# Two ScalarE steps of a weight chunk issued half a block later, and a 384-column copy given to GpSimd, in an attention and mixture-of-experts kernel

## Chip, cores and metric

The kernel runs on one core of one Trainium2 chip. The metric is the device time of one execution in microseconds (us); the figure given for a kernel is the median of its runs.

## What is computed

The reference is a strided attention followed by two dense stages. Cut to what matters:

```python
def reference(q, k, v, w1, w2, w3, w_out, probs, e_w1, e_w2):
    attn = masked_softmax(q @ k.T / 8) @ v       # 2 batches, 8 heads, 576 rows, 64 per head
    x = attn as a (1152, 512) matrix             # 1152 tokens
    h = ((x @ w1) * (x @ w2)) @ w3               # 512 -> 1024 -> 1024
    x3 = h @ w_out                               # 1024 -> 512
    p = probs / (probs.sum(-1) + 1e-9)
    return sum(p[:, e:e+1] * (relu(x3 @ e_w1[e]) @ e_w2[e]) for e in range(4))
```

## The kernel before

TensorE multiplies in a rounded 32-bit format, so every operand is split into a high part (the rounded value) and a low part (the rest), and each product is three matmuls (L305 high by high, L306 and L307 the two mixed terms). The weights w1, w2, w_out and w3 arrive as 64-bit numbers and are turned into 32-bit ones on the chip.

**Weight chunks.** There are 20 of them, in this order: eight of w1 and w2 together (c_w12), four of w_out, eight of w3. A chunk passes through these steps, each on 128 x 1024 elements:

- a DMA loads it (L140, SyncE's queue); it is issued by load_next, which add calls, so that the load of the chunk two places on is issued behind this chunk's add;
- ScalarE: round_up (L144, works on the low words), then magnitude (L149, writes the tile t). These are the "first two ScalarE steps" of the change, called the **words** below;
- VectorE: clamp (L185, reads and writes t), shift (L188), sign (L191), add (L195, needs the low words of L144);
- the split: split_hi (L203, ScalarE), then split_lo (L232, VectorE).

The generator work() (L260 to L291) issues these steps in a fixed order for one chunk after another. Each call of advance takes it one yield further. The four yields of a chunk c are: split_hi of the chunk before and clamp of c; split_lo of the chunk before and shift of c; sign of c; the words of the chunk after c, then add of c.

**Blocks.** The products a = x @ w1 and b = x @ w2 are made in 32 units (16 for each batch; a unit is one of eight column groups ft by one half, 288 tokens, of a batch). ab_block (L578) issues a unit in two halves. First half: 12 matmuls for a and a ScalarE copy out of PSUM to the tile ab (L601). Second half: 12 matmuls for b and the VectorE product of it with ab (L603). The rest of the unit is issued during the next unit: split_hi (L549, ScalarE, reads the product of L603) at the start of the next unit's first half, split_lo (L553, VectorE) at the start of its second half. Each half has one PSUM bank, taken in turn from five (pool ps). A bank is free again when L601 or L603 has read it.

run_unit (L881 to L898) sets the order, once per half:

```python
for _ in range(2):
    next(rest, None)      # L549 or L553 of the unit before
    next(block)           # matmuls, then L601 or L603
    if done >= 2:
        advance(1)        # one step of work()
```

Every engine's instructions run in the order in which the program issues them. In the second batch (units 16 to 31) steps of work() begin again with unit 18: the clamp of chunk w_out 1 stands in its first half. From there a chunk's four yields fill two units, clamp always in the first half of an even unit and add (with the next chunk's words) in the second half of an odd one. The chunks clamped in units 18, 20, 22, 24, 26, 28 and 30 are w_out 1, 2, 3 and w3 0, 1, 2, 3.

After units 17, 20 and 23 ab_split (L555) splits a pair of whole products of the first batch: ScalarE L562 and L563, VectorE L566 and L567. ab_place (L522) reserves a buffer for split products; for the last pair of the second batch, at the start of unit 28, it also copies 2 x 192 columns of the first batch's products from one buffer to another (L529, ScalarE). They are read in the third stage, by x3_block.

After unit 31 come eight products w3 by w_out (wc_tile, L618; accumulators from the same five banks; product number it needs chunk w3 it), then x3_block and the experts.

Of the kernel before, what the change touches and what calls it, by code (L numbers as in the profile page):

```python
# [8 lines left out]
F32 = mybir.dt.float32  # L9
# [18 lines left out]
MID = 384  # L28
# [16 lines left out]
def kernel(  # L45
# [13 lines left out]
    nc = tc.nc  # L59
# [192 lines left out]
    def load_next(held=False):  # L252
        nonlocal loaded
        if loaded < len(stream):
            stream[loaded].raw_load(held)
            loaded += 1
            for load in rest_loads.pop(loaded, ()):
                load()

    def work():  # L260


        wide = stream[2:20]
        before = None
        for c, after in zip(wide, wide[1:] + [None]):
            if before:
                while live > 14:
                    yield False
                before.split_hi()
            c.clamp()  # L270
            yield True
            if before:
                before.split_lo()
            c.shift()
            yield True
            c.sign()
            yield True
            if after:
                after.round_up()
                after.magnitude()  # L280
            c.add()
            yield True
            before = c
        while live > 14:
            yield False
        before.split_hi()
        yield True
        before.split_lo()
        yield True
        for w in c_e:  # L290
            yield from w.work()  # L291

    worker = work()

    def advance(n=1):

        return all([next(worker, False) for _ in range(n)])

    def need(c, part=0):
        while not (c.done if part == 0 else c.done1 if part == 1 else c.done2):  # L300
            assert advance()
# [218 lines left out]
    parts_of, middle, whole = {}, {}, {}  # L520

    def ab_place(b, pair):  # L522
        both = big[b].tile([P, 4 * S], F32R, tag="big", name="ab_parts")
        parts_of[b, pair] = both[:, :4 * MAIN].rearrange("p (x k n) -> p x k n", x=2, k=2)
        rest = both[:, 4 * MAIN:].rearrange("p (x n) -> p x n", x=2)
        if pair == 3 and b == 0:
            middle[pair, 0] = rest[:, :, MID // 2:]
        elif pair == 3:
            nc.scalar.copy(rest[:, :, :MID // 2], middle[pair, 0].bitcast(F32))  # L529
        middle[pair, 1 - b] = rest  # L530

    def ab_pieces(b, ft, t0, n):
# [22 lines left out]
    def ab_split(pair):  # L555

        ab_place(0, pair)
        if (1, pair) not in parts_of:
            ab_place(1, pair)
        ab, main = whole.pop(pair), parts_of[0, pair]  # L560
        for k in range(2):
            nc.scalar.copy(middle[pair, k][:, 0, :MID // 2], ab[:, k, MAIN:])  # L562
        nc.scalar.copy(main[:, 0], ab[:, :, :MAIN])  # L563
        for k in range(2):
            x = middle[pair, k][:, :, :MID // 2]
            nc.vector.tensor_tensor(out=x[:, 1], in0=ab[:, k, MAIN:], in1=x[:, 0].bitcast(F32), op=ALU.subtract)  # L566
        nc.vector.tensor_tensor(out=main[:, 1], in0=ab[:, :, :MAIN], in1=main[:, 0].bitcast(F32), op=ALU.subtract)  # L567
# [10 lines left out]
    def ab_block(b, ft, n):  # L578
        t = slice(b * S + n * HB, b * S + n * HB + HB)
        pair, late = ft // 2, b == 0 and ft < 6  # L580
        ab = tmp.tile([P, HB], F32, tag="pT", name="ab")
        if n == 0 and ft % 2 == 0:
            if late:
                if pair < 2:
                    parts = big[pair].tile([P, 2, 2, S], F32, tag="big", name="ab_f32")
                    whole[pair] = parts[:, 0]
                    if pair:
                        whole[2] = parts[:, 1]
            elif (b, pair) not in parts_of:
                ab_place(b, pair)  # L590
        if late:
            full = whole[pair][:, ft % 2, n * HB:n * HB + HB]
        else:
            full = ab
            pieces = ab_pieces(b, ft, n * HB, HB)
        for w in range(2):
            acc = bank("ab_acc")[:, :HB]
            for k in range(4):
                mm3(acc, c_w12[ft].parts((w * 4 + k) * P, P), (x_hi[:, k, t], x_lo[:, k, t]), k == 0, k == 3)
            if w == 0:  # L600
                nc.scalar.copy(ab, acc)  # L601
            else:
                nc.vector.tensor_tensor(out=full, in0=acc, in1=ab, op=ALU.mult)  # L603
            yield
        if late:
            return
        split_hi(pieces, ab)
        yield
        split_lo(pieces, ab)
        yield  # L610
# [132 lines left out]
    class Step:  # L743
# [22 lines left out]
        def add(self, out, acc, b):  # L766
            nc.vector.tensor_tensor(out=out, in0=acc, in1=b, op=ALU.add)  # L767

        def first(self, work):

            n = self.half.n
# [6 lines left out]
            self.product(b, "s2", "t2")  # L778
            self.add(u2, b, u1)
            work(1)  # L780
            self.product(c, "s3", "t3")
            self.add(u3, c, u2)
# [58 lines left out]
    def load_probs():  # L841
        den = const.tile([P, NTT], F32, name="den")
        nc.sync.dma_start(out=pn, in_=probs)
        nc.vector.tensor_reduce(out=den, in_=pn, axis=mybir.AxisListType.X, op=ALU.add)
        nc.vector.tensor_scalar_add(den, den, 1e-9)
        nc.vector.reciprocal(den, den)
        nc.vector.tensor_tensor(out=pn, in0=pn, in1=den.unsqueeze(2).to_broadcast([P, NTT, E]), op=ALU.mult)
# [4 lines left out]
    with tc.manual_schedule():  # L852
# [24 lines left out]
        rest = iter(())  # L877
# [3 lines left out]
        def run_unit():  # L881

            nonlocal done, rest
            b, ft, i = units[done]
            if done >= 2:
                need(c_w12[ft])
            block = ab_block(b, ft, i)
            for _ in range(2):
                next(rest, None)
                next(block)  # L890
                if done >= 2:
                    advance(1)
                if waiting:
                    waiting.pop().slots_exps()
            rest = block
            done += 1
            if b == i == 1:
                c_w12[ft].free()  # L898
# [139 lines left out]
        while done < 16:  # L1038
            if done == 3:
                need(c_w12[2])  # L1040
            run_unit()
            if done in (4, 5, 6, 7, 8, 10, 11, 13, 14):
                attend(1, next(steps))
            if done == 6:
                zero.whole_split()
        load_probs()
        while done < 32:
            run_unit()
            if done in (18, 21, 24):
                ab_split({18: 0, 21: 1, 24: 2}[done])  # L1050
        for _ in rest:
            pass
        for i in (loaded, loaded + 3):
            if i < 20:
                stream[i].spare = xp, "x_lo"
# [5 lines left out]
        for it in range(8):  # L1061
# [9 lines left out]
            if i is not None:  # L1071
                c = wc[i]
# [4 lines left out]
        c = None  # L1077
# [132 lines left out]
```

## Time and profile before

| what | us |
|---|---|
| median of 3 runs (lowest, highest) | 618.53 (618.53, 618.88) |
| the profiled execution | 618.26 |
| its span in the profile | 616.1 |
| TensorE busy in the span | 609.8 |
| VectorE busy | 443.1 |
| ScalarE busy | 280.6 |
| GpSimd busy | 9.9 |

The profiled execution lies 0.27 us below the median and 2.16 us above its own span. In the profile PE is TensorE's matmuls, PEld its weight loads, DVE VectorE, ACT ScalarE, POOL GpSimd, SP SyncE; L12 is line 12 of the kernel. A matmul's shown duration overlaps that of the next one, so its rate is read from start to start.

### The profile page before, as it was taken

The page shows a single profiled execution, that of the slowest core. Times are in us where ns is not written, and L with a number is a line of the kernel's source. Part 1 is how long each engine was busy: PE and PEld are TensorE (multiplying, and loading weights), DVE is VectorE, ACT ScalarE, POOL GpSimd, SP SyncE. Part 2 cuts the span into 40 slices and gives each one's busy share as a digit, 9 for nine tenths or more (in the row PEclk, how much of TensorE's full clock was granted, in tenths as well). Part 3 has the DMA queues.
Part 4 walks back from the last instruction along what each step waited for, and adds up shares of the span by engine and source line. Part 5 has one row for each costly group of instructions (what it writes and reads, how often), then busy time and mean ns, then how long its engine had stood idle before and what let it go on. Part 6 is the DMA issues. An engine that isn't in the chain of part 4 may idle for free.

```text
span 616.1 us, 11131 instructions
## 1 busy us (share of the span) xinstructions
PE 609.8 (99%) x4488; PEld 555.9 (90%) x4488; DVE 443.1 (72%) x811; ACT 280.6 (46%) x568; POOL 9.9 (2%) x33
## 2 busy tenths in 40 slices
PE   8999999999999999999999999999999999999997
PEld 5799999998889999998899988999889898989997
DVE  4899987998863237777877987887766665755843
ACT  3879966665733134333433333434343333333320
POOL 4100000000000000000000000000000000000000
PEclk9999999999999999999999999999999999999999
DMA  9896330334522202333545334435585557464411
GB/s 272 321 325 185 139 138 2 111 132 172 202 68 102 86 19 69 137 138 136 199 153 194 128 149 172 167 142 212 178 318 202 213 192 248 162 234 176 156 51 68
DMA packets 28510, 99.63 MB, mean 162 GB/s; under 512 B 2660, under 2 KB 6316, under 8 KB 26028
## 3 DMA queue, kind: packets, MB, share of 16 engines
q1 hardware_dynamic: 27916, 98.34, 44.5%
q8 instruction: 35, 0.57, 0.4%
q10 hardware_dynamic: 544, 0.59, 0.3%
q14 instruction: 15, 0.12, 0.1%
HBM read 79.78 MB, written 19.14 MB: 161 GB/s over the span
## 4 chain that ended last, share of the span: by engine, by line
PE 90%; DVE 4%; ACT 3%; DMA 2%; issue 1%; DVEq 0%; ACTq 0%; SPq 0%
PE g_acc L305 11%; PE g_acc L306 11%; PE g_acc L307 11%; PE m_a L307 4%; PE m_a L306 4%; PE m_a L305 4%; PE ab_acc L305 3%; PE ab_acc L307 3%; PE ab_acc L306 3%; PE m_b L306 3%; PE m_c L305 3%; PE m_c L306 3%; PE m_b L305 3%; PE x_acc L305 3%; PE m_c L307 3%; PE m_b L307 3%
## 5 line engine op out<-in xcount | busy, mean ns | idle before, releaser
L761 ACT ACTIVATE h_hi<-u 128x320 fp32r<-128x320 f32 (+1 forms) x128 | 56.9, 445 | 188.9 <-DVE u L767 188.9
L305 PE MATMUL g_acc<-w_hi,h_hi 128*128 128x512 f32 (+1 forms) x296 | 114.3, 386 | 0.0
L306 PE MATMUL g_acc<-w_lo,h_hi 128*128 128x512 f32 (+1 forms) x296 | 114.2, 386 | 0.0
L307 PE MATMUL g_acc<-w_hi,h_lo 128*128 128x512 f32 (+1 forms) x296 | 113.7, 384 | 0.0
L700 DVE TENSOR_TENSOR w_lo<-raw,w_hi 128x768 fp32r<-128x768 f32 x64 | 69.3, 1084 | 12.3 <-ACT w_hi L698 12.3
L767 DVE TENSOR_TENSOR u<-m_b,u 128x320 f32<-128x320 f32 (+1 forms) x96 | 40.7, 451 | 50.4 <-PE m_b L307 50.4
L305 PE MATMUL ab_acc<-x_hi,w_hi 128*128 128x288 f32 x240 | 71.6, 298 | 0.4 <-ACT ab L601 0.2
L307 PE MATMUL ab_acc<-x_hi,w_lo 128*128 128x288 f32 x240 | 70.7, 295 | 0.0
L306 PE MATMUL ab_acc<-x_lo,w_hi 128*128 128x288 f32 x240 | 70.7, 294 | 0.0
L307 PEld LDWEIGHTS g_acc<-w_hi,h_lo 128*128 128x128 f32 x296 | 55.6, 188 | 11.6
L305 PEld LDWEIGHTS g_acc<-w_hi,h_hi 128*128 128x128 f32 x296 | 55.8, 188 | 8.0
L306 PEld LDWEIGHTS g_acc<-w_lo,h_hi 128*128 128x128 f32 x296 | 55.7, 188 | 7.6
L763 DVE SCALAR_TENSOR_TENSOR h_lo<-u,h_hi 128x320 fp32r<-128x320 f32 (+1 forms) x128 | 57.6, 450 | 3.6 <-ACT h_hi L761 1.1
L698 ACT CAST w_hi<-raw 128x768 fp32r<-128x768 f32 x64 | 59.9, 936 | 0.0
L305 PEld LDWEIGHTS ab_acc<-x_hi,w_hi 128*128 128x128 f32 x240 | 45.0, 188 | 1.0 <-ACT ab L601 0.5
L306 PEld LDWEIGHTS ab_acc<-x_lo,w_hi 128*128 128x128 f32 x240 | 45.0, 188 | 0.0
L307 PEld LDWEIGHTS ab_acc<-x_hi,w_lo 128*128 128x128 f32 x240 | 45.0, 188 | 0.0
L306 PE MATMUL m_b<-b_t,s_hi 128*128 128x320 f32 (+1 forms) x128 | 37.9, 296 | 0.0
L767 DVE TENSOR_TENSOR u<-m_a,u 128x320 f32<-128x320 f32 (+1 forms) x64 | 28.8, 449 | 11.6 <-PE m_a L307 11.6
L700 DVE TENSOR_TENSOR s_lo<-raw,s_hi 128x1024 fp32r<-128x1024 f32 x16 | 19.6, 1225 | 24.3 <-ACT s_hi L698 24.3
L767 DVE TENSOR_TENSOR u<-m_c,u 128x320 f32<-128x320 f32 (+1 forms) x64 | 28.9, 452 | 4.5 <-PE m_c L307 3.9
L777 ACT COPY u<-m_a 128x320 f32<-128x320 f32 (+1 forms) x32 | 12.7, 398 | 42.4 <-PE m_a L307 42.4
(180 smaller groups left out, 1384.6 us busy)
## 6 DMA issues: line engine op xcount, KB each, us to landing
raw<-in_e_dram SPq DMA_DIRECT2D x32, 1024.0 KB, 4.9
raw<-in_w3T_dram SPq DMA_DIRECT2D x8, 1024.0 KB, 4.9
stored<-s_hi SPq DMA_DIRECT2D x16, 512.0 KB, 2.6
stored<-s_lo SPq DMA_DIRECT2D x16, 512.0 KB, 2.6
s_hi<-stored SPq DMA_DIRECT2D x16, 512.0 KB, 3.7
s_lo<-stored SPq DMA_DIRECT2D x16, 512.0 KB, 4.9
raw<-in_w_dram SPq DMA_DIRECT2D x7, 1024.0 KB, 7.2
raw<-in_w_out_dram SPq DMA_DIRECT2D x4, 1024.0 KB, 5.0
```

Source lines behind the costliest of these rows:

```text
L305: mm(acc, lh, rh, start=first, stop=False)
L306: mm(acc, lh, rl, start=False, stop=False)
L307: mm(acc, ll, rh, start=False, stop=last)
L698: nc.scalar.copy(dst[0], src)
L700: nc.vector.tensor_tensor(out=dst[1], in0=src, in1=dst[0].bitcast(F32), op=ALU.subtract)
L761: nc.scalar.activation(hi, src, AF.Relu)
L763: nc.vector.scalar_tensor_tensor(out=lo, in0=src, scalar=0.0, in1=hi.bitcast(F32), op0=ALU.max, op1=ALU.subtract)
L767: nc.vector.tensor_tensor(out=out, in0=acc, in1=b, op=ALU.add)
L777: nc.scalar.copy(u1, a)
```

## The change

Between unit 16 and the end of unit 31 the words of the next chunk are not issued at once ahead of add, but put into a list; run_unit empties it behind the next half's matmuls and its PSUM copy or product, ahead of that half's step of work(). The last words in the list are issued after the rest of unit 31. The copy of 384 columns in ab_place is issued on GpSimd instead of ScalarE.

```diff
+    later_words = None
+
+    def flush():
+        while later_words:
+            c = later_words.pop()
+            c.round_up()
+            c.magnitude()
@@ work()
             c.sign()
             yield True
-            if after:
+            if after and later_words is not None:
+                later_words.append(after)
+            elif after:
                 after.round_up()
                 after.magnitude()
             c.add()
@@ ab_place()
         elif pair == 3:
-            nc.scalar.copy(rest[:, :, :MID // 2], middle[pair, 0].bitcast(F32))
+            nc.gpsimd.tensor_copy(out=rest[:, :, :MID // 2], in_=middle[pair, 0].bitcast(F32))
@@ run_unit()
                 next(block)
+                flush()
                 if done >= 2:
                     advance(1)
@@ the order of the stages
         load_probs()
+        later_words = []
         while done < 32:
             run_unit()
...
         for _ in rest:
             pass
+        flush()
+        later_words = None
```

## Rows read from the trace of the kernel before

**Rows 1.** The page, part 2: TensorE's busy tenths in 40 slices of 15.4 us.

```profile
PE   8999999999999999999999999999999999999997
```

**Rows 2.** Waits of 78 to 180 us: total, times, longest (us).

```profile
ACT raw L144 <- DMA raw<-in_w3T_dram: 12.0, 5, 2.9
...
PE ab_acc L305 <- ACT ab L601: 0.2, 1, 0.2
```

**Rows 3.** Timeline of PE, 136.9 to 142.4 us: start us, us, instruction, idle before.

```profile
136.98 0.29 PE L307 MATMUL ab_acc<-x_hi,w_lo 128*128 128x288 f32 x1
137.51 0.40 PE L305 MATMUL ab_acc<-x_hi,w_hi 128*128 128x288 f32 x1 [0.24 <-ACT ab L601]
...
142.39 0.49 PE L305 MATMUL wc_acc<-w_hi 128*128 128x512 f32 x1
```

**Rows 4.** Timeline of ACT in the second batch's units.

```profile
102.39 0.40 ACT L601 COPY ab<-ab_acc 128x288 f32<-128x288 f32 x1 [0.57 <-PE ab_acc L307]
102.68 1.18 ACT L144 ACTIVATE raw<-raw 128x1024 int32<-128x1024 uint32 x1
...
105.51 0.40 ACT L601 COPY ab<-ab_acc 128x288 f32<-128x288 f32 x1
...
128.30 0.43 ACT L549 CAST ab_parts<-ab 128x288 fp32r<-128x288 f32 x1 [0.88 <-DVE ab L603]
128.64 0.39 ACT L601 COPY ab<-ab_acc 128x288 f32<-128x288 f32 x1
...
134.22 1.21 ACT L144 ACTIVATE raw<-raw 128x1024 int32<-128x1024 uint32 x1 [2.62 <-DMA raw<-in_w3T_dram]
135.29 1.13 ACT L149 ACTIVATE t<-raw 128x1024 f32<-128x1024 f32 x1
...
136.64 0.52 ACT L529 CAST ab_parts<-ab_parts 128x384 fp32r<-128x384 f32 x1
137.06 0.40 ACT L601 COPY ab<-ab_acc 128x288 f32<-128x288 f32 x1
```

**Rows 5.** Timeline of DVE in the same units and just behind them.

```profile
99.42 0.68 DVE L185 TENSOR_SCALAR t<-t 128x1024 f32<-128x1024 f32 x1
...
104.61 0.45 DVE L603 TENSOR_TENSOR ab<-ab_acc,ab 128x288 f32<-128x288 f32 x1
...
106.11 0.68 DVE L185 TENSOR_SCALAR t<-t 128x1024 f32<-128x1024 f32 x1
...
112.25 0.45 DVE L603 TENSOR_TENSOR ab<-ab_acc,ab 128x288 f32<-128x288 f32 x1
...
123.04 0.68 DVE L185 TENSOR_SCALAR t<-t 128x1024 f32<-128x1024 f32 x1
...
127.81 0.45 DVE L603 TENSOR_TENSOR ab<-ab_acc,ab 128x288 f32<-128x288 f32 x1
128.18 1.22 DVE L195 CUSTOM_DVE_ANT_0 t<-raw,t 128x2048 uint16<-128x2048 uint16 x1
129.31 0.69 DVE L185 TENSOR_SCALAR t<-t 128x1024 f32<-128x1024 f32 x1
...
141.88 0.45 DVE L603 TENSOR_TENSOR ab<-ab_acc,ab 128x288 f32<-128x288 f32 x1
...
151.48 0.69 DVE L185 TENSOR_SCALAR t<-t 128x1024 f32<-128x1024 f32 x1
```

**Rows 6.** Timeline of POOL: the nearest instructions to the new copy.

```profile
9.63 0.83 POOL L450 TENSOR_TENSOR p_ring<-p_ring,rec 128x384 f32<-128x384 f32 x1 [4.29 <-DVE rec L446]
...
18.61 0.91 POOL L450 TENSOR_TENSOR p_ring<-p_ring,rec 128x432 f32<-128x432 f32 x1 [0.91 <-DVE rec L438]
...
19.52 1.09 POOL L450 TENSOR_TENSOR p_ring<-p_ring,rec 128x432 f32<-128x432 f32 x1
```

**Rows 7.** Timelines of DVE and PE: the last w3 chunk, and who needs it.

```profile
177.63 1.22 DVE L232 TENSOR_TENSOR w_lo<-t,w_hi 128x1024 fp32r<-128x1024 f32 x1 [1.12 <-ACT w_hi L203]
...
181.05 0.39 PE L307 MATMUL wc_acc<-w_hi,w_lo 128*128 128x512 f32 x1
```

## The prediction

> **What bounds the kernel now.** I read the page first. TensorE is busy in 99% of the span, and the slices show nine tenths or more from the second slice to the last but one [rows 1]. So the time falls only where TensorE gets a gap less, and rises only where it gets one more. The waits of the stretch that the change touches come next: in 100 us TensorE's matmuls wait for ScalarE once, for the PSUM copy of L601; the long waits, 12.0 us in five times, are those of the first word (L144) for a w3 load [rows 2]. TensorE's timeline shows what that one gap costs. The last three halves of the second batch, 36 matmuls, run from 137.51 to the first w3-by-w_out product at 142.39, so 0.136 us each; before them 137.51 - 136.98 = 0.53 us pass, so 0.39 us are lost [rows 3]. ScalarE's timeline says why: L144 stood at the head of the queue until its load landed (2.62 us), and L149, L549, L529 and L601 behind it; the copy that gave the bank back ended at 137.46 [rows 4]. **All that the change can win in this stretch is that 0.39 us.**
>
> The second thing to read is how near the other engines are to that limit. Each half has one of five banks, so TensorE is at most four halves ahead of the copies and products that empty them. It starts the first w3-by-w_out product at 142.39, 0.06 us behind the end of the product of unit 29 (141.88 + 0.45 = 142.33) [rows 3, 5]: that product needs the same bank. So TensorE is already as far ahead as it may be, VectorE empties banks just in time, and **any delay of VectorE in this stretch goes to TensorE one to one**.
>
> **Part 1: the words behind L601.** Removed are the waits of L549 and L601 behind the words. No instruction is added to ScalarE, and loads keep their place behind add (L195) on SyncE's queue. What changes is who waits for the words. Clamp needs L149. Before, the words were issued in the same half as add, ahead of the next half's L549; ScalarE had them to do while VectorE was at shift, sign and the product, and clamp followed add directly: add at 128.18, clamp at 129.31 [rows 5]. Now the words stand behind L549 and L601 of the next half, and L549 needs the VectorE product L603 of the same half as add. Between L603 and clamp there is now a serial chain through ScalarE, while VectorE has only add to do.
>
> The tail from the start of L603 to the start of clamp, step by step: L603 0.45; handoff to ScalarE 128.30 - 128.26 = 0.04; L549 to L601 128.64 - 128.30 = 0.34; L601 to L144 102.68 - 102.39 = 0.29; L144 to L149 135.29 - 134.22 = 1.07; L149 1.13; handoff 0.04 [rows 4, 5]. Sum 3.36. Before it was 129.31 - 127.81 = 1.50 where no load was late, so 1.86 us more. The loads are not in the way any more: a load issued at the end of add at 129.40 had landed at 134.22, 4.82 us later, and in the new order L144 comes some 6.5 us behind that add.
>
> The other part of a cycle, from clamp to the second L603, is VectorE's own work without gaps: 127.81 - 123.04 = 4.77, and 112.25 - 106.11 = 6.14 in the cycle that holds the split of a whole pair [rows 5]. A new cycle is 4.77 + 3.36 = 8.13 us, where TensorE needs 48 x 0.136 = 6.5 for the same two units.
>
> Now the sum, clamp by clamp. The clamp of w_out 1 at 99.42 and the product of unit 19 at 104.61 stay, since the first words in the list come behind them [rows 5].
> - w_out 2: L601 at 105.51, as before because TensorE gives it its data about then, + 0.29 + 1.07 + 1.13 + 0.04 = 108.04 (before 106.11) [rows 4, 5].
> - w_out 3: + 6.14 + 3.36 = 117.54.
> - w3 0: + 8.13 = 125.67 (before 123.04). Here the second split's VectorE work, 6.14 - 4.77 = 1.37, fits into the gap of 1.86 ahead of clamp and costs nothing; its two ScalarE steps run while ScalarE waits for L603.
> - w3 1: 133.80. w3 2: 141.93.
> - The product of unit 29: 141.93 + 4.77 = 146.70, where it was 141.88 [rows 5].
>
> So **TensorE starts the w3-by-w_out products 4.8 us later.** This is the whole difference at that point: the 0.39 us gap of before lies within the 4.8, and the new lag shows as several gaps of about 0.5 to 1.2 us, from the time on when the four halves of lead are used up (about unit 26).
>
> Behind unit 31 the words are issued behind the last L549, with no L601 between. Clamp of w3 3 comes at 141.93 + 8.13 = 150.06; of w3 4 at 150.06 + 4.77 + 3.36 - 0.29 = 157.9, before 151.48 [rows 5]: 6.4 later, while TensorE is 4.8 later. What covers the difference of 1.6? The last chunk w3 7 was ready at 177.63 + 1.22 = 178.85 and its low part is first used at 181.05, a reserve of 2.20 [rows 7]. From there on the order of work is that of before. So nothing is added; if the reserve fails by half a microsecond TensorE waits that long more. TensorE has no gaps behind this stage in which the lag could be made up [rows 1].
>
> **Part 2: the copy on GpSimd.** It takes 0.42 us (137.06 - 136.64) from ScalarE's chain at unit 28 [rows 4]; the new chain above is reckoned without it. No POOL copy is in the trace; the nearest row, an operation with two inputs on as many columns, took 0.83 us, and one of 432 columns took 0.91 and 1.09 on two occasions [rows 6]. POOL has nothing else queued there. It copies early, when its buffer is free behind the second split, and its result is read only in the third stage, tens of us later, so it costs nothing itself. What is open is whether it holds up a VectorE step of the chain. Bounds from rows: nothing below, and above one whole copy, 0.83 us, since the chain has a single VectorE step waiting at a time. I take 0.15, the size of the spread between the two like POOL rows (1.09 - 0.91 = 0.18).
>
> The Trainium skill, "SBUF — State Buffer", section "Who interferes with whom", says that VectorE and GpSimd share a port pair under a lock, and that one in a two-port mode fully blocks the other for an instruction. By that rule the sum would take the upper bound, 0.83 in place of 0.15, if the copy starts just ahead of clamp. The rows show a spread of 0.18 only, and no run here shows the lock.
>
> **Sum.** 4.82 + 0.15 = about 5.0. Against the profiled execution: 618.26 + 5.0 = 623.3. The median of the runs is 0.27 above it, so 618.53 + 5.0 = **623.5 us**.
>
> **The rivals.**
> 1. *Not slower.* The reordering does what waits alone suggest: L549 and L601 no longer stand behind a late load, banks come back earlier, and VectorE's gap ahead of clamp lies in slack. The time would be 618.53 - 0.39 = 618.1, within what counts as the same. For it speaks the only TensorE wait of the stretch [rows 2, 3]. It decides by one comparison: if L149 ends before add does. Add ends at 128.18 + 1.22 - 127.81 = 1.6 us behind the start of L603, the words 3.3 us behind it. That speaks against it, and so does the product of unit 29, which already empties its bank at the last moment. Chance 0.08, with 0.02 more that something I don't see makes it faster by over 0.2%.
> 2. *Slower by more.* The lag of 6.4 us at w3 4 isn't covered, because the w3 chunks behind it lose a further one or two microseconds (the reserve of 2.20 shrinks to 0.6 by my sum), or the copy blocks a step of the chain for its length. 0.5 to 1.5 more: 624.3 to 625.2. Chance 0.2.
> 3. *Slower by less.* Part of the lag is made up, by a shorter tail (L601 need not always wait for L549's product where VectorE was early) or by VectorE in the w3 stage, where its reserve is large for the first products. 1 to 3 us less: 620.5 to 622.5. Chance 0.1.
>
> The forecast itself, 622.7 to 624.2, has 0.6.
>
> **How the numbers follow.** About 0.2% (1.2 us) is what a measurement of this kernel can tell from no change. The gain is limited to 0.39 us, so faster has 0.02; same is rival 1, 0.08; the rest, 0.9, is slower. The range goes from 621.6, which takes in the upper half of rival 3, to 625.2, the end of rival 2.
>
> **What would show it.** In the profile after: L144 directly behind L601 in every second unit and no more waiting for w3 loads in the units; idle time of VectorE ahead of clamp, 1.5 to 1.9 us, released by L149, some six times; clamps of w3 0, 1, 2 near 125.7, 133.8 and 141.9; several waits of TensorE for L601 and L603, in sum about 5 us, from about 123 us on; the first w3-by-w_out product near 147.2; no waits behind it; POOL's copy about 0.5 to 0.8 us long. Wrong it would be if clamp followed add directly, or if TensorE's gaps summed to under 1 us; or, with the lag as forecast, if the w3 stage won it back.

## The result, and the profile after

The changed kernel takes 624.25 us (median of 5 runs, 622.88 to 624.41) against 618.53: 1.0088 times as long, 95% interval 1.0073 to 1.0103, so 5.7 us more. Forecast were 623.5 and 5.0. A second set of six runs (below) has 622.83, 4.2 us above the runs beside it, 1.0059 with an interval of 1.0038 to 1.008. The forecast lies between the two.

In the code after, the lines behind work() stand ten higher: L559 is the old L549, L611 is L601, L613 is L603, L315 is L305, L539 is the moved copy L529. L144, L149, L185, L203 and L232 kept their numbers.

ScalarE's timeline of the changed kernel, one cycle (start us, us, instruction, idle before it):

```profile
140.60 0.43 ACT L559 CAST ab_parts<-ab 128x288 fp32r<-128x288 f32 x1 [2.98 <-DVE ab L613]
140.94 0.39 ACT L611 COPY ab<-ab_acc 128x288 f32<-128x288 f32 x1
141.23 1.14 ACT L144 ACTIVATE raw<-raw 128x1024 int32<-128x1024 uint32 x1
142.26 1.13 ACT L149 ACTIVATE t<-raw 128x1024 f32<-128x1024 f32 x1
143.27 1.05 ACT L203 CAST w_hi<-t 128x1024 fp32r<-128x1024 f32 x1
```

VectorE's timeline of the changed kernel: the clamps, and the products and add that stand ahead of one of them:

```profile
100.99 0.69 DVE L185 TENSOR_SCALAR t<-t 128x1024 f32<-128x1024 f32 x1
...
109.63 0.69 DVE L185 TENSOR_SCALAR t<-t 128x1024 f32<-128x1024 f32 x1 [1.86 <-ACT t L149]
...
118.99 0.69 DVE L185 TENSOR_SCALAR t<-t 128x1024 f32<-128x1024 f32 x1 [1.72 <-ACT t L149]
...
127.11 0.84 DVE L185 TENSOR_SCALAR t<-t 128x1024 f32<-128x1024 f32 x1 [0.35 <-ACT t L149]
...
135.34 0.70 DVE L185 TENSOR_SCALAR t<-t 128x1024 f32<-128x1024 f32 x1 [1.72 <-ACT t L149]
...
140.12 0.45 DVE L613 TENSOR_TENSOR ab<-ab_acc,ab 128x288 f32<-128x288 f32 x1
140.49 1.22 DVE L195 CUSTOM_DVE_ANT_0 t<-raw,t 128x2048 uint16<-128x2048 uint16 x1
143.42 0.70 DVE L185 TENSOR_SCALAR t<-t 128x1024 f32<-128x1024 f32 x1 [1.72 <-ACT t L149]
...
148.20 0.45 DVE L613 TENSOR_TENSOR ab<-ab_acc,ab 128x288 f32<-128x288 f32 x1
```

GpSimd's timeline of the changed kernel has the copy alone:

```profile
126.89 0.51 POOL L539 CAST ab_parts<-ab_parts 128x384 fp32r<-128x384 f32 x1 [106.74 <-DVE ab_parts L577]
```

Read ScalarE's and VectorE's timelines together. In [rows 4] ScalarE stood with a word at the head of its queue, waiting for a load; now it stands 2.98 us with L559 at the head, waiting for VectorE's product, and the words can only follow. The product starts at 140.12, L559 at 140.60, then come L611, L144 and L149, and clamp starts at 143.42: 3.30 us, most of it through ScalarE. VectorE has only add to do meanwhile, and its idle time of 1.72 us ahead of clamp, released by L149, is what [rows 5] does not have.

TensorE's waits in its timeline, same kernel; the column in brackets is idle time:

```profile
128.74 0.40 PE L315 MATMUL ab_acc<-x_hi,w_hi 128*128 128x288 f32 x1 [1.03 <-DVE ab L613]
...
132.54 0.40 PE L315 MATMUL ab_acc<-x_hi,w_hi 128*128 128x288 f32 x1 [0.35 <-DVE ab L613]
...
136.82 0.40 PE L315 MATMUL ab_acc<-x_hi,w_hi 128*128 128x288 f32 x1 [0.86 <-DVE ab L613]
...
140.62 0.40 PE L315 MATMUL ab_acc<-x_hi,w_hi 128*128 128x288 f32 x1 [0.33 <-DVE ab L613]
...
144.91 0.40 PE L315 MATMUL ab_acc<-x_hi,w_hi 128*128 128x288 f32 x1 [0.86 <-DVE ab L613]
...
148.71 0.50 PE L315 MATMUL wc_acc<-w_hi 128*128 128x512 f32 x1 [0.34 <-DVE ab L613]
```

The one gap of [rows 3] has become six, each released by a VectorE product that empties a bank. Their idle times sum to 3.77 us; the shown durations run over into the gaps, so the true loss is larger and is read from the places of two events. From the clamp of w_out 1 to the first w3-by-w_out product it is 148.71 - 100.99 = 47.72 us; before, 142.39 - 99.42 = 42.97 [rows 3, 5]. **The stretch is 4.75 us longer.** The stage behind it is not. The first x3 matmul, TensorE's timelines, before and after:

```profile
186.04 0.34 PE L305 MATMUL x_acc<-ab_parts,w_hi 128*128 128x384 f32 x1
```

```profile
192.36 0.34 PE L315 MATMUL x_acc<-ab_parts,w_hi 128*128 128x384 f32 x1
```

From the first w3-by-w_out product to there it is 43.65 us in both profiles.

One thing in this execution is not the change's. The clamp of w_out 1 stands at 100.99 and not at 99.42, 1.57 us later, though nothing ahead of it was changed. TensorE in windows of 2 us (length, busy and instructions, granted clock, DMA share, GB/s):

```profile
18.00:20.00 2.00, 1.63 (x63) 1.00 0.64 254
20.00:22.00 2.00, 2.00 (x52) 0.55 0.84 238
22.00:24.00 2.00, 2.00 (x17) 0.60 0.97 346
```

TensorE had a gap of 0.84 us, which the profile calls issue, at 17.5 us; from a little behind 20 us to a little ahead of 24 us the granted clock was at its lower level (0.50 in the half microseconds from 20.5 to 23.5). TensorE's first matmul of the blocks then starts at 25.37 in place of 23.76. The second profile of the same kernel, below, has a clock of 1.00 there.

### The profile page after: what moved, and what is told of

It reads as the page before. It is cut to its first block, busy times and chain, and to the rows that moved or that the text cites. A ratio compares the mean times of both kernels' runs of the same rounds, so it can differ in the third digit from the quotient of the medians.

```text
span 622.4 us, 11133 instructions
## 1 busy us (share of the span) xinstructions
PE 612.4 (98%) x4488; PEld 557.3 (90%) x4488; DVE 443.7 (71%) x811; ACT 279.8 (45%) x567; POOL 10.3 (2%) x34
## 4 chain that ended last, share of the span: by engine, by line
PE 89%; DVE 5%; ACT 3%; issue 2%; DMA 1%; ACTq 0%; DVEq 0%
PE g_acc L315 11%; PE g_acc L316 11%; PE g_acc L317 11%; PE m_a L317 4%; PE m_a L316 4%; PE m_a L315 4%; PE ab_acc L315 3%; PE ab_acc L317 3%; PE ab_acc L316 3%; PE m_b L316 3%; PE m_c L315 3%; PE m_c L316 3%; PE x_acc L315 3%; PE m_b L315 3%; PE m_c L317 3%; PE m_b L317 3%
## 5 line engine op out<-in xcount | busy, mean ns | idle before, releaser
L315 PE MATMUL g_acc<-w_hi,h_hi 128*128 128x512 f32 (+1 forms) x296 | 114.3, 386 | 0.0
L315 PE MATMUL ab_acc<-x_hi,w_hi 128*128 128x288 f32 x240 | 72.0, 300 | 3.6 <-DVE ab L613 3.4
L315 PEld LDWEIGHTS g_acc<-w_hi,h_hi 128*128 128x128 f32 x296 | 55.8, 188 | 8.0
L315 PEld LDWEIGHTS ab_acc<-x_hi,w_hi 128*128 128x128 f32 x240 | 45.0, 188 | 5.1 <-DVE ab L613 4.6
```

What stands on the lines that cost most here:

```text
L315: mm(acc, lh, rh, start=first, stop=False)
```

## Experiments

All stretches below run from the clamp of w_out 1 to the first w3-by-w_out product in the kernel's own profile, which leaves differences in the first 99 us out. The kernel before has one profile; where ScalarE still waits for w3 loads, as it does there, a load's landing alone moved a clamp by 0.36 us (see copy only), so differences of 0.3 in the last column show nothing by themselves.

| kernel | median us | ratio to before, 95% | stretch us | against before |
|---|---|---|---|---|
| before | 618.53 | | 42.97 | |
| changed | 624.25 | 1.0073 to 1.0103 | 47.72 | +4.75 |
| changed, again | 622.83 | 1.0038 to 1.008 | 47.71 | +4.74 |
| words only | 623.28 | 1.0046 to 1.0093 | 47.98 | +5.01 |
| copy only | 618.82 | 0.9983 to 1.0014 | 43.27 | +0.30 |
| first word only | 618.20 | 0.9978 to 1.0011 | 42.67 | -0.30 |
| second word only | 618.93 | 0.9996 to 1.0022 | 43.79 | +0.82 |
| words from unit 24 | 620.85 | 1.0023 to 1.0051 | 45.64 | +2.67 |
| changed, eight banks | 624.16 | 1.0077 to 1.0107 | 42.47 | -0.50 |
| copy eight times | 619.91 | 1.0009 to 1.003 | 44.07 | +1.10 |

The medians of before that stood beside the two series of experiments were 618.64 and 618.71.

**The changed kernel again**, without an edit.

> The changed kernel once more, for a second profile. In the first profile the clamp of w_out 1 stood at 100.99 us, 1.57 later than in the kernel before, though nothing ahead of it was changed: there the granted clock fell to 0.5 between about 20 and 24 us behind a gap of 0.84 us on TensorE. From that clamp on everything lay within 0.2 us of the prediction. Theory: those 1.57 us belong to that execution and not to the change. Then in this profile the stretch from the clamp of w_out 1 to the first w3-by-w_out product is 48.8 - 101.0 + 100 within 0.2 us of the first one (148.7 minus 101.0, 47.7 us, where before it was 142.39 minus 99.42, 43.0), while the place of that clamp may be anywhere from 99.4 to 101.0. Rival: the shifted code of the changed kernel itself makes the early gap, always; then the clamp stands near 101.0 again with the clock at 0.5 ahead of it. Median expected 623.3 to 624.4.

(The sum in its middle is written out badly; the figures meant are the 47.7 and 43.0.) The clamp of w_out 1 stands at 99.29, the clock at 1.00 all through, and the stretch is 47.71, the first profile's within 0.01. So the fall of the clock belonged to the first profiled execution, and the words and the copy cost 4.7 us. The median, 622.83, is 0.5 below what was expected. The other three high runs of the first set (624.41, 624.25, 623.97) did not have that fall: their mean granted clocks are 1.000, 1.000 and 0.999, where the profiled execution has 0.997. Why they lie over 1 us above the second set's median is not shown, since only the profiled execution left a trace. The first 99 us differ between executions for other reasons as well: two kernels below have that clamp at 100.8 and 100.9 with the clock at 1.00 up to there, and in both TensorE waited 0.73 us for the low part of a weight chunk near 42.7 us. That is why the stretch is compared.

**Words only**, the copy left on ScalarE:

```diff
-            nc.gpsimd.tensor_copy(out=rest[:, :, :MID // 2], in_=middle[pair, 0].bitcast(F32))
+            nc.scalar.copy(rest[:, :, :MID // 2], middle[pair, 0].bitcast(F32))
```

> The words deferred, the copy left on ScalarE. Theory: the whole loss is that of the tail through ScalarE; the copy adds 0.42 us to one of the cycles (unit 28), and the clamp of w3 0, which was 0.84 us long beside GpSimd's copy, is 0.69 again. So 0.3 us slower than the changed kernel: stretch from the clamp of w_out 1 to the first w3-by-w_out product 48.0 us, time 623.6 to 624.6. Rival: the copy on GpSimd makes a good part of the loss; then this kernel is 1 us or more faster than the changed one.

Stretch 47.98, 0.27 longer than the changed kernel's. The clamp of w3 0 is 0.69 us long without the copy beside it, and the gap ahead of the clamp in the cycle of unit 28 is 2.12 in place of 1.72. The loss is the words'; moving the copy gives 0.27 of it back. The median, 623.28, is 0.45 above the changed kernel's second one and 0.3 below the times that were expected.

**Copy only**: the kernel before with the copy on GpSimd (the opposite of the diff above).

> The kernel before with the copy of 384 columns on GpSimd and nothing else. Theory: it takes 0.42 us from ScalarE's chain ahead of L601 of unit 28, so that TensorE's gap of 0.39 us at 137 us is gone; nothing waits for the copy. 618.1 us, no difference that can be measured. Rival (the port that VectorE and GpSimd share): a VectorE step beside the copy is blocked for the length of the copy, 0.5 us, and the gap stays: 618.5 to 619.0.

No difference that can be measured, but the reason given for it was half wrong: TensorE's gap stayed, as the rival had it, and 618.82 lies in the rival's range. GpSimd's and VectorE's timelines of this kernel:

```profile
123.91 0.83 POOL L529 CAST ab_parts<-ab_parts 128x384 fp32r<-128x384 f32 x1 [103.25 <-DVE ab_parts L567]
```

```profile
123.69 0.69 DVE L185 TENSOR_SCALAR t<-t 128x1024 f32<-128x1024 f32 x1
124.30 0.76 DVE L553 TENSOR_TENSOR ab_parts<-ab,ab_parts 128x288 fp32r<-128x288 f32 x1
124.97 0.45 DVE L603 TENSOR_TENSOR ab<-ab_acc,ab 128x288 f32<-128x288 f32 x1
```

The copy was issued within a clamp and took 0.83 us where it takes 0.51 in the changed kernel; L553 was issued within the copy and took 0.76 where 0.45 is its length elsewhere. L553 ends 0.32 us behind the copy. L603, which reads PSUM and SBUF, has its usual 0.45. So VectorE lost 0.31 us, most of the 0.42 that ScalarE's chain won; and ScalarE's wait for the w3 0 load was 3.04 us, where it was 2.68 before, which is no work of the copy. Together they outweigh the gain (-0.42 + 0.31 + 0.36 = +0.25; the stretch has +0.30). TensorE's gap stayed (0.54 us of idle time at 138.09, behind L601). The Trainium skill, "SBUF — State Buffer", section "Who interferes with whom", has that a VectorE instruction in a two-port mode, or with both inputs in SBUF, and a GpSimd one that reads SBUF exclude each other for whole instructions. These two timelines agree, nearly: a copy of 0.51 us behind the clamp's end (124.38) would end at 124.89 and ended at 124.74, and an L553 of 0.45 behind the copy's end would end at 125.19 and ended at 125.06.

**The copy eight times over**, in the kernel before:

```diff
-            nc.scalar.copy(rest[:, :, :MID // 2], middle[pair, 0].bitcast(F32))
+            for _ in range(8):
+                nc.gpsimd.tensor_copy(out=rest[:, :, :MID // 2], in_=middle[pair, 0].bitcast(F32))
```

> The kernel before with the copy on GpSimd issued eight times over, the same columns each time. In the runs so far one copy took 0.50 us beside a clamp that took 0.82 in place of 0.69, and 0.83 us where it started within a clamp, with the product split L553 behind it at 0.76 in place of 0.45. Theory (each blocks the other for a whole instruction): some eight VectorE steps are held up by 0.15 to 0.5 us each, VectorE has no slack there, and TensorE starts the w3-by-w_out products 2 to 4 us later: 620.5 to 622.5 us. Rival (those two steps were chance, or the two engines only slow each other a little): below 619.2 us.

Between the two: 1.2 us slower. The eight copies took 7.95 us, 0.51 to 1.44 each. VectorE's timeline beside them:

```profile
124.57 0.76 DVE L554 TENSOR_TENSOR ab_parts<-ab,ab_parts 128x288 fp32r<-128x288 f32 x1
125.25 0.45 DVE L604 TENSOR_TENSOR ab<-ab_acc,ab 128x288 f32<-128x288 f32 x1
125.61 1.21 DVE L232 TENSOR_TENSOR w_lo<-t,w_hi 128x1024 fp32r<-128x1024 f32 x1
126.75 0.99 DVE L188 TENSOR_SCALAR t<-t 128x1024 int32<-128x1024 int32 x1
127.77 1.40 DVE L191 SCALAR_TENSOR_TENSOR t<-raw,t 128x1024 int32<-128x1024 int32 x1
129.10 1.13 DVE L554 TENSOR_TENSOR ab_parts<-ab,ab_parts 128x192 fp32r<-128x192 f32 x2
```

Lengthened are L554 (by 0.31, and by 0.61 for the pair), L188 (0.30), L191 (0.17), and behind these rows the next clamp (0.99 at 131.69, by 0.30); L604 and this L232 (1.21) are not. The cycle is 7.72 us (clamps at 123.97 and 131.69) in place of 6.27, and TensorE is 1.10 later. VectorE's loss does reach TensorE, though not one to one, and my 2 to 4 us took too many steps as blocked: eight copies of 0.51 us would take 4.1 and took 7.95, so GpSimd did much of the waiting itself.

**Only the first word deferred**, the copy on GpSimd:

```diff
             if after and later_words is not None:
+                after.magnitude()
                 later_words.append(after)
@@ flush()
             c.round_up()
-            c.magnitude()
```

> Only the first word (L144) is deferred; the second (L149) keeps its place ahead of add; the copy is on GpSimd. Theory: clamp needs L149 alone, so the serial chain L603, L549, L601, L144, L149, clamp is not formed; L144 is needed only by add, three steps later. No lag of clamp: clamps of w3 0 and w3 1 near 123 and 129 us (beside a clamp of w_out 1 at 99.4), no gap of VectorE released by L149 over 0.8 us, no TensorE gap at 137 us: 618.1 us, same as before. Rival: any deferring of ScalarE work behind L549 and L601 costs in proportion to its length (half of the change's 5 us): 620.5 to 621.

The theory holds: this word, about as long as the other, costs nothing behind the same L611, and clamp does not read what it writes. TensorE has no gap at all in the units; the first product starts 42.67 us behind the clamp of w_out 1, 0.30 earlier than before. By the first x3 matmul that is gone again: the w3 stage takes 43.95 in place of 43.65, with a wait for the low part (L232) of chunk w3 6. One gap of clamp behind L149 was a little over the 0.8 named (0.98 at 145.64, where L149 had waited for a load). The 618.2 us can't be told from the kernel before.

**Only the second word deferred**:

```diff
             if after and later_words is not None:
+                after.round_up()
                 later_words.append(after)
@@ flush()
-            c.round_up()
             c.magnitude()
```

> Only the second word (L149) is deferred; the first (L144) keeps its place. Theory: the tail is 3.36 - 1.07 = 2.29 us and not 3.36, a cycle 7.06 where VectorE's own work is 6.27: clamps near 123.8, 130.9, 138.0 (beside a clamp of w_out 1 at 99.4), the first w3-by-w_out product at 143.2 in place of 142.39: 619.0 to 619.5 us. L144 again waits for loads ahead of L549. Rival (cost in proportion to the work deferred, half of the change's): 620.8 to 621.3.

In its profile the clamp of w_out 1 stands at 100.84, 1.42 later than before. Less that, the clamps are at 123.8, 130.9 and 137.9 and the product at 143.2, as the sum said, and each clamp has a gap of about 0.7 us:

```profile
132.28 0.70 DVE L185 TENSOR_SCALAR t<-t 128x1024 f32<-128x1024 f32 x1 [0.71 <-ACT t L149]
```

The median, 618.93, is 0.2 above before and 0.07 below the low end; the interval (0.9996 to 1.0022) holds both no change and the sum. The tail is what costs, with its length: 3.30 us give 4.7, 2.3 give 0.8. So the two words together cost far more than each alone: the first, which costs nothing by itself, stands ahead of the second in the tail once both are moved. VectorE's cycle of 7.1 us here is 0.5 above the 6.5 that TensorE needs for two units; that of 8.1 us with both words is 1.6 above it.

**Words deferred from unit 24 on**:

```diff
-        later_words = []
         while done < 32:
+            if done == 24:
+                later_words = []
             run_unit()
```

> The words are deferred only from unit 24 on: those of w3 1, 2, 3 and 4, and not those of w_out 2, w_out 3 and w3 0. Theory: cycles of 8.13 us from the clamp of w3 0 at 123.04: w3 1 131.17, w3 2 139.30, product of unit 29 144.07 where it was 141.88, so 2.2 us less what GpSimd's copy adds or saves: 620.4 to 621.0 us. Rival (the loss comes with the first deferral and not by the cycle, or from the late w3 stage): about 618.3 or about 623.3.

620.85 us, as forecast. The gaps of 1.72 us begin with the clamp of w3 1. The stretch is 2.67 longer, 0.5 more than the 2.2 of the sum: the clamp of w3 0 comes 0.28 later behind that of w_out 1 than before, ahead of any deferred word, and the copy holds up L563 (0.76 in place of 0.45). The loss comes cycle by cycle.

**The changed kernel with eight banks**:

```diff
-            acc = bank("ab_acc")[:, :HB]
+            h = 4 * ft + 2 * n + w
+            if b == 1 and h % 8 >= 5:
+                acc = ps_sc.tile([P, 512], F32, tag="sc", name="ab_acc")[:, :HB]
+            else:
+                acc = bank("ab_acc")[:, :HB]
```

> The changed kernel, with the second batch's halves on eight PSUM banks in turn in place of five (the three of the scores' pool are idle there), so that TensorE may be seven halves ahead of the copies and products that empty them. The tail through ScalarE stays as it is. Theory (VectorE's lag goes to TensorE wherever the two meet next): the gaps in the units vanish and the first w3-by-w_out product starts at about 142.0 (beside a clamp of w_out 1 at 99.4), as in the kernel before; but the w3 chunks are 6.4 us late and the reserve of the last one is 2.2, so that TensorE waits for split_lo (L232) in the w3 stage, 2 to 4.5 us in sum: 620.5 to 622.5 us. Rival (only the banks cost): the whole loss is gone, 618.1 us.

The mechanism is as the theory has it and the price is not: 624.16 is 1.7 above the range. TensorE has no gap in the units; it starts the w3-by-w_out products 42.47 us behind the clamp of w_out 1, earlier than the kernel before. Then it meets the late w3 chunks (TensorE's timeline of this kernel):

```profile
159.44 0.50 PE L315 MATMUL wc_acc<-w_hi 128*128 128x512 f32 x1 [0.79 <-ACT w_hi L203]
...
160.70 0.50 PE L317 MATMUL wc_acc<-w_hi,w_lo 128*128 128x512 f32 x1 [0.53 <-DVE w_lo L232]
...
166.05 0.39 PE L316 MATMUL wc_acc<-w_lo,w_hi 128*128 128x512 f32 x1
168.87 0.79 PE L317 MATMUL wc_acc<-w_hi,w_lo 128*128 128x512 f32 x1 [2.43 <-DVE w_lo L232]
169.46 0.63 PE L315 MATMUL wc_acc<-w_hi 128*128 128x512 f32 x1
169.89 0.63 PE L316 MATMUL wc_acc<-w_lo,w_hi 128*128 128x512 f32 x1
```

From the first of these products to the first x3 matmul it is 49.56 us in place of 43.65, 5.9 more. The waits for L203 and L232 were expected, 2 to 4.5 in sum; beyond the usual 0.23 between two starts the three took 4.2. What was not expected: behind the gap of 2.43 us the matmuls start 0.43 us apart in place of 0.23, and the windows show the clock at its lower level:

```profile
168.00:170.00 2.00, 1.13 (x3) 0.61 0.02 8
170.00:172.00 2.00, 2.00 (x7) 0.54 0.00 0
```

The seven matmuls from 168.87 to 171.95 took 3.08 us in place of 7 x 0.23 = 1.6, so the clock added 1.5 to the 5.9. The same lag spread over six gaps of at most 1.03 us left the clock at 1.00 in the changed kernel. So the banks were where VectorE's lag showed, not its cause.

## Why the prediction was right

- **What bounds the kernel.** TensorE had 0.39 us to win and VectorE no slack. Right in the main: with five banks, every kernel that lengthened VectorE's cycle clearly lengthened the stretch. One to one was too strong: eight copies lengthened a cycle by 1.45 us and TensorE lost 1.10.
- **The tail.** 3.36 us forecast; 140.12 to 143.42 is 3.30. VectorE's gap, 1.5 to 1.9 forecast, is 1.72 to 1.86; the second split's work lies in it at w3 0, where 0.35 is left.
- **The clamps.** Less the 1.57 us of the early stage, w_out 2 to w3 2 stand at 108.06, 117.42, 125.54, 133.77 and 141.85 (sum: 108.04, 117.54, 125.67, 133.80, 141.93), the product of unit 29 at 146.63 (146.70). In the second profile, too, each cycle is within 0.2 us.
- **TensorE's gaps.** The total was right, 4.75 against 4.82 and the copy's 0.15. They began later: the first ends at 128.74, which is 127.2 less the 1.57, and not at about 123. All six were released by L613 and none by L611.
- **The w3 stage.** The reserve of 2.20 covered the lag; no waits behind it. It was near: the last low part is ready at 187.04 and used at 187.38, 0.34 left where the sum had 0.6. Eight banks, where TensorE comes earlier, shows that the lag was there.
- **The copy.** 0.15 was taken for a step of VectorE held up by it; the clamp of w3 0 took 0.84 in place of 0.69. That the size is right is luck: the spread of two old POOL rows had nothing to do with it, and the upper bound of 0.83 did not come. The copy started 0.22 us ahead of the clamp and ended at 127.40, so 0.29 of its 0.51 us lay beside the clamp. In the profiles where it lies so the clamp takes 0.82 to 0.84; with the second word only the copy ends at 125.19, the clamp starts at 125.20, and it takes its 0.69. In the old order of ScalarE's work the copy costs 0.31.
- **The median.** 624.25 is 0.75 above the forecast and 0.05 above the narrower band of 622.7 to 624.2; the second set is 0.7 below the forecast. The 1.57 us of low clock in the attention, which nothing in the change concerns, belong to the profiled execution alone, and what lifts the other runs of the first set is open. That 623.5 lies between the two sets is in part luck.
- **Two slips that decided nothing.** The words come some 7.7 us behind the add that issues their load by the sum's own terms, and 7.6 in the profile (133.62 to 141.23), not some 6.5. Rival 2's end would be 623.5 + 1.5 = 625.0, not 625.2.

Rival 1, not slower, fell as its own test said: add ended at 141.71, L149 at 143.39. Rival 2's time begins 0.05 above the median and two of the five runs lie in it, but neither of its mechanisms came: the w3 stage lost nothing, and the copy lengthened one clamp by 0.15. Of rival 3 nothing came: the lag was not made up, and the tail was 0.06 us shorter than forecast. No version here beats the kernel before by a measurable amount; the best, the first word alone deferred, could win no more than TensorE's 0.39 us, and the 0.30 that it won in the units was lost in the w3 stage.

## What to carry to other kernels

A wait for a late load at the head of an in-order queue is not a loss by itself: ask what the work behind it and the work that needs it wait for in each order. Moving an instruction behind one that waits for another engine puts that engine's latency into every consumer of the moved one; add up the new cycle and compare it with the bound engine's. Steps that are moved together are to be priced together: here the one that clamp doesn't read costs nothing that could be measured, the one that it reads 0.8 us of stretch, and both 4.7, since the free one then lies in the chain ahead of the other.

## What the runs showed of the hardware

- A GpSimd copy of 384 columns takes 0.50 to 0.51 us where it doesn't start within a VectorE step (four profiles) and 0.83 to 0.84 where it starts 0.2 us into a clamp (copy only, first word only, from unit 24). A VectorE step with both inputs in SBUF took 0.76 in place of 0.45 behind it, and one that reads PSUM kept its 0.45.
- TensorE's clock fell to its lower level behind one gap of 2.43 us, and for some 3 us matmuls cost 0.43 us apiece in place of 0.23. Behind gaps of up to 1.03 us in the changed kernel's units, and of 1.26 in words only, it stayed at 1.00. In the attention, with its small matmuls, it once fell at about 20 us, with a gap of 0.84 ahead of it, and did not in the second profile. What made it fall there is not shown: with the words deferred from unit 24 on TensorE was idle for as long between 16 and 20 us (0.84 and 0.85 us), and the clock stayed at 1.00.
